# Key-value sums in four parts of 128 small matmuls, with MLP units between the parts, in a fused linear-attention and SwiGLU kernel

## The chip, the cores and the metric

The kernel runs on one core of a Trainium2 chip. The metric is device time in microseconds (us) of one execution; lower is better. Five engines work side by side, each through its own list of instructions in order: TensorE (PE in the profile; its weight loads are PEld), VectorE (DVE), ScalarE (ACT), GpSimd (POOL) and SyncE (SP), which here issues all DMA transfers.

## The reference

For one sequence of S = 2048 tokens with D = 640 features, two branches are added to the input. Both start from the same layer-normed input.

```python
xn = _layernorm(x)                     # x: (1, 2048, 640)
# branch A: linear attention, H = 32 heads of Dh = 20
q, k, v = split(xn @ wqkv)
pq = einsum("bhsd,hdf->bhsf", q, w_phi);  pk = einsum("bhsd,hdf->bhsf", k, w_phi)
phi_q = concat([softmax(pq), softmax(-pq)]);  phi_k = concat([softmax(pk), softmax(-pk)])
kv  = einsum("bhsf,bhsd->bhfd", phi_k, v);    z = einsum("bhsf->bhf", phi_k)
o   = einsum("bhqf,bhfd->bhqd", phi_q, kv) / (einsum("bhqf,bhf->bhq", phi_q, z) + 1e-6)
A   = o @ wo
# branch B: SwiGLU, F = 1536
B   = (silu(xn @ w1) * (xn @ w3)) @ w2
out = x + A + B
```

The key-value sums `kv` and `z` run over all tokens. Per head they are a matrix of 40 by 20 and a vector of 40.

## The kernel before

**Tiles.** Tokens lie in T = 16 tiles of 128 and in NB = 4 blocks of 512; D is cut into DC = 5 chunks of 128, F into FC = 12. Matrices are bf16, sums in PSUM are f32. PSUM has eight banks; every unit of work asks for one or two of them (`banks(n)`), those that become free first.

**Stages.** Layer norm and transposition of x; then, tile by tile, keys (with w_phi folded into the weights, `Wkp`) and values; the exponentials of the keys land in `ekt`, are summed on VectorE and scaled on GpSimd (`k_norm`); v is kept in `v2`, with a column of ones behind each head, so that z comes out of the same sums as kv. Then the key-value sums (`kv_sum`), their store into a block layout (`kv_store`, into `KVc`), and for every token tile `q_tok`: 40 small groups of matmuls against `KVc`, the division on VectorE, and a transposed DMA into `oT`. The query projections (`q_proj`) run a block ahead. The MLP is cut into 48 units (`mlp`, one block of tokens by one chunk of F): five matmuls for the gate and five for the up projection, each 128x512, in two banks; a tanh on ScalarE; two steps on VectorE, which leave the result in `hT` and free the banks. `out_tile` adds both branches in PSUM, 34 matmuls of 320 columns per token tile, and SP writes the tile out.

**The key-value sums.** Lines 554 to 565. Eight heads' columns n, 16 token tiles t and four row groups r give 8 x 16 x 4 = 512 matmuls in one unit. Each loads its own weights, 128 x 21 (a head of v and the column of ones), and streams 40 columns (both halves of `ekt` of this head). They go into 320 columns of one bank, and one ScalarE instruction (`kv_copy`) brings these to `stg`. In the profile the matmuls read `PS<-ekt,v`, that copy `stg<-PS,eps`, the MLP's matmuls `PS<-xnT,w_s` (w1 and w3; w2 has the name `w_s`, too), those of `q_proj` `PS<-xnT,Wqp`, those of `q_tok` `PS<-KVc,EqT`.

**What sets the order.** The program is planned before it is built. Each stream of work (norms, transposes, attention, MLP, outputs and so on, line 820) is a generator that yields units, or nothing while it has to wait. The planner (lines 823 to 858) keeps a modelled time for each engine, takes the unit that can start first by its model (`P.ready` for units with TensorE work), and appends its instructions to the engines' lists; a unit is never cut. The costs in the code (as 0.0055 per small matmul at line 563) serve this model alone. On the chip each engine goes through its list in order, and semaphores carry the dependences that `find_deps` found. The stream `attention` yields all projections, then `kv_masks`, `kv_sum` (line 781), `kv_store`, and the load of w2, which goes where `ekt` lay; MLP units of the last block wait for this (line 807).

Of the kernel before, what the change touches and what calls it, by code (L numbers as in the profile page):

```python
# [11 lines left out]
DH = 20  # L12
F = 1536
T = S // 128
# [232 lines left out]
def bass_parallel_sum__linear_kernel_hedgehog__glu_gated_swiglu__prompt_kernel(  # L247
# [10 lines left out]
):  # L258
    bf = DT.bfloat16
    LAG = 4.0  # L260
    f32 = DT.float32
    P = _Program(nc)

# [11 lines left out]
    def new(name, shape, dtype, offset=None):  # L275
        size = mybir.dt.size(dtype)
        for n in shape[1:]:
            size *= n
        return P.sbuf(name, shape, dtype, region(size) if offset is None else offset)
# [10 lines left out]
    eps = new("eps", [128, 8], f32)  # L290
# [43 lines left out]
    stg = new("stg", [128, 2, 160], bf, RW + 1344)  # L334
# [10 lines left out]
    def bank(k, cols=512, off=0, rows=128):  # L345
        return PS[0:rows, k * 512 + off:k * 512 + off + cols]
# [5 lines left out]
    def mm(o, l, r, start, stop, shared=False, cost=None):  # L352
        n = free(r)
        P.op("PE", "matmul", [o], [l, r], (o, l, r),
             dict(start=start, stop=stop, skip_group_check=shared),
             cost=max(n / 2400 + 0.003, 0.055) if cost is None else cost)
# [5 lines left out]
    def free(ap):  # L362
        n = 1
        for s in ap.shape[1:]:
            n *= s
        return n
# [132 lines left out]
    def fold_mm(which, dc, k):  # L499
        first = [True, True]  # L500
        for e in range(DC):
            h0, h1 = heads_of_chunk(e)
            lo, hi = DH * h0, DH * (h1 + 1)
            for q in range(2):
                a, b = max(lo, 320 * q), min(hi, 320 * q + 320)
                if a < b:
                    mm(bank(k + q, b - a, a - 320 * q), wqkT[:, which * DC + e, 128 * dc:128 * dc + 128],
                       BDc[:, e, a - lo:b - lo], first[q], e == DC - 1 or (q == 0 and e == 2), True)
                    first[q] = False
        if which:  # L510
            evac(Wkp[:, dc, :].rearrange("p (b c) -> p b c", c=320), bank2(k, 320))
        else:
            evac(Wqp[:, dc, :].rearrange("p (i b r j) -> p b r i j", b=2, r=2, j=32),
                 bank2(k, 320).rearrange("p b (r i j) -> p b r i j", r=2, j=32))
# [8 lines left out]
    def v_half(t, q, k):  # L523
        for i in range(DC):
            mm(bank(k, 320), xnT[:, i, t * 128:(t + 1) * 128], wv[:, i, 320 * q:320 * q + 320],
               i == 0, i == DC - 1)
        act(v2[:, t, 336 * q:336 * q + 336].rearrange("p (h c) -> p h c", c=21)[:, :, 0:DH],
            bank(k, 320).rearrange("p (h c) -> p h c", c=DH), ACT.Copy)

    def v_tile(t, k):  # L530
        proj(t, wv, k)
        pv = bank2(k, 320).rearrange("p b (h c) -> p b h c", c=DH)
        act(v2[:, t, :].rearrange("p (b h c) -> p b h c", b=2, c=21)[:, :, :, 0:DH], pv, ACT.Copy)

    def k_tile(t, k):
        proj(t, Wkp, k)
        pk = bank2(k, 320)
        for sg in range(2):
            act(ekt[:, t, sg, :].rearrange("p (b c) -> p b c", c=320), pk, ACT.Exp,
                1.0 if sg == 0 else -1.0)  # L540
# [10 lines left out]

    def kv_sum(k):
        for n in range(8):
            for t in range(T):
                for r in range(4):
                    h = 8 * r + n
                    o = PS[32 * r:32 * r + DH + 1, k * 512 + 40 * n:k * 512 + 40 * n + 40]
                    edge = r == 0 and (n == 0 and t == 0 or n == 7 and t == T - 1)  # L560
                    mm(o.rearrange("p (s f) -> p s f", s=2), v2[:, t, 21 * h:21 * h + DH + 1],
                       ekt[:, t, :, DH * h:DH * h + DH], t == 0, t == T - 1, True,
                       (0.1 if edge else 0.0) + 0.0055)
        kv_copy(stg[:].rearrange("p s (n f) -> p n s f", f=DH),
                bank(k, 320).rearrange("p (n s f) -> p n s f", s=2, f=DH), eps[:, 0:1])

    def kv_copy(o, i, e):
        n = free(o)
        P.op("ACT", "activation", [o], [i, e], (o, i, ACT.Identity), dict(bias=e), cost=0.17 + n / 1200)
# [22 lines left out]
    def q_proj(b, fc, k):  # L592
        for i in range(DC):
            mm(bank(k), Wqp[:, i, fc * 128:(fc + 1) * 128], xnT[:, i, b * 512:(b + 1) * 512],
               i == 0, i == DC - 1)
        act(EqT[b % 2][:, 0, fc, :], bank(k), ACT.Exp)
        act(EqT[b % 2][:, 1, fc, :], bank(k), ACT.Exp, -1.0)
# [51 lines left out]
    def load_xres(t):  # L649
        P.dma("SP", xres[:, t % 4, :], x_t[:, t, :])  # L650
# [23 lines left out]
    def banks(n):  # L674

        def free_at(k):
            return max([o.end for i in range(k, k + n) for o in P.bank.get(("P", i), {}).values()],
                       default=0.0)
        return min(range(0, 8, n), key=free_at)

    done = dict.fromkeys(("w", "ln", "t", "f", "k", "n", "kv", "q", "o", "h"), 0)
# [70 lines left out]
    def attention():  # L752
        def v(t):
            return lambda: v_tile(t, banks(2))

        yield warm_up
        for t in range(4):
            while done["t"] <= t:
                yield None
            for q in range(2):  # L760
                yield lambda t=t, q=q: v_half(t, q, banks(1))
        while done["f"] < 1:
            yield None
        for t in range(T):
            while done["t"] <= t:
                yield None
            yield lambda t=t: k_tile(t, banks(2))
            done["k"] = t + 1
            if t >= 4:
                yield v(t)  # L770
            if 9 <= t < 14:
                while done["f"] < 2:
                    yield None
                yield lambda dc=t - 9: fold_mm(0, dc, banks(2))
        yield lambda: P.dma("SP", wo_s[:], A_wo.rearrange("(c p) d -> p c d", p=128))
        for fc in range(DC):
            yield lambda fc=fc: q_proj(0, fc, banks(1))
        while done["n"] < T:
            yield None
        yield kv_masks  # L780
        yield lambda: kv_sum(banks(1))
        yield kv_store
        done["kv"] = 1
        yield lambda: P.dma("SP", w2_s[:], B_w2.rearrange("(c p) d -> p c d", p=128))
        yield lambda: (load_xres(0), load_xres(1))
        for b in range(NB):
            for j in range(4):
                t = 4 * b + j
                while done["o"] < t - 2:
                    yield None  # L790
                yield lambda t=t: q_tok(t, 0)
                done["q"] = t + 1
                if b + 1 < NB:
                    for fc in range((5 * j + 3) // 4, (5 * j + 8) // 4):
                        yield lambda b=b, fc=fc: q_proj(b + 1, fc, banks(1))
# [22 lines left out]
    MLPS = 7  # L818
    URGENT = {0: 4.0, 4: 4.0, 6: 4.0}
    streams = [norms(), transposes(), fold_k(), attention(), k_norms(), loads(), o_transposes(), mlps(), outs()]  # L820
    n = len(streams)
    heads, alive = [None] * n, [True] * n
    while any(alive):
        best = None
        for i in range(n):
            if heads[i] is None and alive[i]:
                s = next(streams[i], StopIteration)
# [12 lines left out]
            if any(o.eng == "PE" for o in ops):  # L840
                at = max(P.ready(ops), P.free["PE"] + 0.15)
                if i == MLPS and P.free["DVE"] > P.free["PE"] + LAG:
                    rank = n
# [10 lines left out]
        i, ops, after = best[2:]  # L854
# [65 lines left out]
```

## Time and profile before

| | us |
|---|---|
| median of 3 runs | 281.02 |
| lowest and highest run | 280.66, 281.38 |
| the profiled execution | 280.1 |
| its span, first to last instruction | 278.4 |
| mean granted TensorE clock in it | 0.988 |

A run's time is the span and 1.7 us around it. The profile is of one execution. Its rows give the engine, the operation, the tiles (output<-inputs), the shape, a count, the busy time and the mean length of one, and then the idle time of the engine just before these instructions, with what ended most of it; "issue" there is a wait for nothing that the profile shows. All instructions come from the helper at line 105, so groups are told apart by their tiles, not their lines. Matmuls are pipelined: one lasts longer than the distance to the next, so starts are counted, not lengths. Some records of matmuls are missing from a trace. The granted clock is TensorE's, 1.00 being full speed.

### The profile page before, as it was taken

What the parts mean: (1) busy time and instruction counts of PE and PEld (TensorE: products, weight loads), DVE (VectorE), ACT (ScalarE), POOL (GpSimd) and SP (SyncE); (2) the same over time, 40 slices, a digit from 0 to 9 for tenths busy, and PEclk for the clock granted to TensorE, in tenths of its full rate; (3) what the DMA queues carried; (4) which work ended last, traced back from release to release, by engine and by line L of the source; (5) the groups of instructions that cost most, each with busy time, mean ns of one, the idle gap of its engine ahead of it and who ended that gap; (6) DMA issues with size and microseconds to landing.
All of it is one profiled execution on the core that took longest, in us unless ns stands there. A gap on an engine that the chain in (4) does not pass through costs nothing.

```text
span 278.4 us, 6314 instructions
## 1 busy us (share of the span) xinstructions
PE 263.4 (95%) x2711; PEld 155.8 (56%) x2735; DVE 179.4 (64%) x306; ACT 104.7 (38%) x196; POOL 60.9 (22%) x99
## 2 busy tenths in 40 slices
PE   6999999999994599999999999999999999999996
PEld 2656666676444344444444444446666666777774
DVE  5469879999561066656666799994665555786212
ACT  2567988887720122232222355451223222100000
POOL 4405496999982000000000100000000000000000
PEclk9999999999999599999999999999999999999999
DMA  6972799630000270000000011120633432253311
GB/s 193 305 214 47 167 318 228 122 117 0 0 0 5 58 279 0 0 2 0 1 0 2 0 26 24 27 47 26 90 80 82 64 93 73 73 116 99 99 46 47
DMA packets 40332, 22.06 MB, mean 79 GB/s; under 512 B 26736, under 2 KB 40304, under 8 KB 40304
## 3 DMA queue, kind: packets, MB, share of 16 engines
q1 hardware_dynamic: 40304, 21.66, 31.8%
q8 instruction: 21, 0.34, 0.5%
q14 instruction: 7, 0.06, 0.1%
HBM read 12.81 MB, written 2.62 MB: 55 GB/s over the span
## 4 chain that ended last, share of the span: by engine, by line
PE 88%; issue 4%; DMA 4%; SPq 2%; DVE 1%; ACT 1%
PE PS L105 88%; DMA wqkT<-in_A_wqkv_dram 4%; SPq L117 2%; DVE S L105 1%; ACT Wkp L105 0%; ACT ekt L105 0%; DVE t L105 0%; DVE rS L105 0%; DVE xres L105 0%; DVE hT L105 0%
## 5 line engine op out<-in xcount | busy, mean ns | idle before, releaser
L105 PE MATMUL PS<-xnT,w_s 128*128 128x512 bf16 x469 | 105.1, 381 | 1.0 <-issue 0.3
L105 PEld LDWEIGHTS PS<-xnT,w_s 128*128 128x128 bf16 x480 | 47.1, 98 | 56.7 <-issue 1.4
L105 DVE SCALAR_TENSOR_TENSOR t<-th,PS 128x512 bf16<-128x512 f32 x48 | 32.8, 683 | 42.7 <-ACT th L105 42.4
L105 PE MATMUL PS<-w_s,hT 128*128 128x320 bf16 (+2 forms) x384 | 54.9, 299 | 0.0
L105 ACT ACTIVATE th<-PS 128x512 f32<-128x512 f32 x48 | 28.7, 599 | 58.7 <-PE PS L105 58.7
L105 PEld LDWEIGHTS PS<-w_s,hT 128*128 128x128 bf16 x384 | 37.6, 98 | 14.6
L105 POOL TENSOR_TENSOR ekt<-ekt,rS 128x640 bf16<-128x640 bf16 x32 | 39.4, 1272 | 4.1 <-DVE rS L105 4.1
L105 DVE TENSOR_TENSOR xres<-PS,xres 128x640 bf16<-128x640 f32 (+2 forms) x17 | 13.4, 786 | 38.9 <-PE PS L105 38.9
L105 DVE SCALAR_TENSOR_TENSOR hT<-t,PS 128x512 bf16<-128x512 bf16 x48 | 33.0, 687 | 1.7
L105 ACT ACTIVATE e_s<-PS 128x64 f32<-128x64 f32 x32 | 6.4, 283 | 52.2 <-PE PS L105 52.2
L105 PE MATMUL PS<-wv,xnT 128*128 128x320 bf16 x160 | 24.7, 299 | 1.0 <-ACT xnT L105 1.0
L105 ACT ACTIVATE EqT<-PS 128x512 bf16<-128x512 f32 x40 | 21.7, 594 | 9.2 <-PE PS L105 9.2
L105 PE MATMUL PS<-wo_s,oT 128*128 128x320 bf16 (+2 forms) x160 | 24.5, 299 | 0.0
L105 DVE TENSOR_TENSOR prod<-PS,g_s 128x1280 bf16<-128x1280 f32 x16 | 23.9, 1491 | 0.6
L105 PE MATMUL PS<-Wkp,xnT 128*128 128x320 bf16 x160 | 23.9, 299 | 0.1
L105 ACT ACTIVATE ekt<-PS 128x640 bf16<-128x640 f32 x32 | 20.9, 720 | 6.3 <-PE PS L105 6.3
L105 DVE TENSOR_REDUCE S<-ekt 128x64 f32<-128x1280 bf16 x16 | 23.1, 1441 | 0.0
L105 PE MATMUL PS<-xnT,Wqp 128*128 128x512 bf16 x87 | 20.9, 379 | 2.0 <-issue 1.9
L105 PEld LDWEIGHTS PS<-wv,xnT 128*128 128x128 bf16 x160 | 15.2, 98 | 7.5 <-ACT xnT L105 1.5
L105 PEld LDWEIGHTS PS<-wo_s,oT 128*128 128x128 bf16 x160 | 15.3, 98 | 7.2
L105 PEld LDWEIGHTS PS<-Wkp,xnT 128*128 128x128 bf16 x160 | 15.4, 98 | 6.5 <-issue 0.3
L105 DVE BATCH_NORM_STATS2 bst<-x_tok 128x6 f32<-128x320 bf16 x32 | 15.3, 478 | 4.9 <-DMA x_tok<-in_A_x_dram 4.3
(52 smaller groups left out, 142.9 us busy)
## 6 DMA issues: line engine op xcount, KB each, us to landing
w_s<-in_B_w_dram SPq DMA_DIRECT2D x6, 640.0 KB, 6.1
xres<-in_A_x_dram SPq DMA_DIRECT2D x16, 160.0 KB, 2.5
out_dram<-xres SPq DMA_DIRECT2D x15, 160.0 KB, 1.8
x_tok<-in_A_x_dram SPq DMA_DIRECT2D x3, 640.0 KB, 6.3
w_s<-in_B_w_dram SPq DMA_DIRECT2D x1, 1920.0 KB, 9.4
wv<-in_A_wqkv_dram SPq DMA_DIRECT2D x2, 400.0 KB, 4.8
wo_s<-in_A_wo_dram SPq DMA_DIRECT2D x1, 800.0 KB, 4.8
x_tok<-in_A_x_dram SPq DMA_DIRECT2D x4, 160.0 KB, 2.9
```

Source lines behind the costliest of these rows:

```text
L105: o = _Op(eng, lambda: m(*args, **kw), r, w, cost)
L117: o = _Op(eng, lambda: m(out, in_), self.regions(in_), self.regions(out), nbytes, True)
```

## The change

`kv_sum` is called four times, with m = 0 to 3, for the columns n = 2m and 2m + 1: 128 matmuls each, over all 16 token tiles and four row groups. Each part goes to 80 columns of whichever bank is free first, and has a copy of its own into its 40 columns of `stg`. Between two parts the attention stream yields nothing until the modelled TensorE time has gone on by 4.2 us (`KV_GAP`), as long as there are MLP units of the first three blocks. The modelled cost of one small matmul goes from 0.0055 to 0.008.

```diff
+    KV_GAP = 4.2
...
-    def kv_sum(k):
-        for n in range(8):
+    def kv_sum(m, k):
+        for n in (2 * m, 2 * m + 1):
             for t in range(T):
                 for r in range(4):
                     h = 8 * r + n
                     o = PS[32 * r:32 * r + DH + 1, k * 512 + 40 * n:k * 512 + 40 * n + 40]
-                    edge = r == 0 and (n == 0 and t == 0 or n == 7 and t == T - 1)
+                    edge = r == 0 and (n % 2 == 0 and t == 0 or n % 2 and t == T - 1)
                     mm(o.rearrange("p (s f) -> p s f", s=2), v2[:, t, 21 * h:21 * h + DH + 1],
                        ekt[:, t, :, DH * h:DH * h + DH], t == 0, t == T - 1, True,
-                       (0.1 if edge else 0.0) + 0.0055)
-        kv_copy(stg[:].rearrange("p s (n f) -> p n s f", f=DH),
-                bank(k, 320).rearrange("p (n s f) -> p n s f", s=2, f=DH), eps[:, 0:1])
+                       (0.1 if edge else 0.0) + 0.008)
+        i, o = bank(k, 80, 80 * m), stg[:, :, 40 * m:40 * m + 40]
+        kv_copy(o.rearrange("p s (n f) -> p n s f", f=DH),
+                i.rearrange("p (n s f) -> p n s f", s=2, f=DH), eps[:, 0:1])
...
         yield kv_masks
-        yield lambda: kv_sum(banks(1))
+        for m in range(4):
+            until = P.free["PE"] + KV_GAP
+            while m and P.free["PE"] < until and done["h"] < 3:
+                yield None
+            yield lambda m=m: kv_sum(m, banks(1))
         yield kv_store
```

On TensorE, from the end of the query projections of the first block to the first `q_tok`, the list is this (rows with - are those of before, rows with + of the changed kernel; ten `PS<-xnT,w_s` are one MLP unit):

```order
 L105 MATMUL PS<-xnT,Wqp 128x512 x25
 L105 MATMUL PS<-xnT,w_s 128x512 x50
-L105 MATMUL PS<-ekt,v_83 21x40 x512
-L105 MATMUL PS<-xnT,w_s 128x512 x300
+L105 MATMUL PS<-ekt,v_83 21x40 x128
+L105 MATMUL PS<-xnT,w_s 128x512 x20
+L105 MATMUL PS<-ekt,v_83 21x40 x128
+L105 MATMUL PS<-xnT,w_s 128x512 x20
+L105 MATMUL PS<-ekt,v_83 21x40 x128
+L105 MATMUL PS<-xnT,w_s 128x512 x20
+L105 MATMUL PS<-ekt,v_83 21x40 x128
+L105 MATMUL PS<-xnT,w_s 128x512 x230
```

Six of the thirty MLP units that followed the sums now stand between the parts, two in each place, and 23 come behind the last part: one unit fewer than before stands ahead of the first `q_tok`.

On ScalarE, at the same place, the copies of the sums stand between the tanh steps of the MLP units (in brackets the engines whose semaphores an instruction waits for):

```order
-L105 ACTIVATE stg<-PS,eps 128x8x2x20 [waits s_PE]
+L105 ACTIVATE stg<-PS,eps 128x2x2x20 [waits s_PE]
+L105 ACTIVATE th<-PS 128x512 [waits s_PE] x2
+L105 ACTIVATE stg<-PS,eps 128x2x2x20 [waits s_ACT,s_PE]
+L105 ACTIVATE th<-PS 128x512 [waits s_PE] x2
+L105 ACTIVATE stg<-PS,eps 128x2x2x20 [waits s_PE]
+L105 ACTIVATE th<-PS 128x512 [waits s_PE] x2
+L105 ACTIVATE stg<-PS,eps 128x2x2x20 [waits s_ACT,s_PE]
 L105 ACTIVATE th<-PS 128x512 [waits s_PE] x3
```

Each copy waits for its own part of the sums, and two of them for an earlier copy on the same engine; the tanh of the unit behind it comes after it in the list.

The unit that was left over comes out on TensorE after the fifth `q_tok`, in front of the sixth:

```order
 L105 MATMUL PS<-xnT,Wqp 128x512 x10
-L105 MATMUL PS<-xnT,w_s 128x512 x10
-L105 MATMUL PS<-wo_s,oT 128x320 x10
-L105 MATMUL PS<-w_s,hT_77 128x320 x24
+L105 MATMUL PS<-xnT,w_s 128x512 x20
 L105 MATMUL PS<-KVc,EqT_82 128x44 x4
```

There two MLP units stand instead of one and an output tile; from here on every output tile comes one place later, so that six of them instead of five follow the last `q_tok`. The lists of VectorE and SP move with this: the transposed DMA of the sixth `o_tok` is issued ahead of the first output tile's residual load and store.

## The prediction

> **What bounds the kernel now.** I read the page's first part and its chain, then the groups of instructions with shapes kept apart, and then, for the place the change touches, the timeline of TensorE and the windows of one microsecond.
>
> ```profile
> span 278.4 us, 6314 instructions
> PE 263.4 (95%) x2711; PEld 155.8 (56%) x2735; DVE 179.4 (64%) x306; ACT 104.7 (38%) x196; POOL 60.9 (22%) x99
> ...
> PE 88%; issue 4%; DMA 4%; SPq 2%; DVE 1%; ACT 1%
> ```
>
> TensorE sets the end: it is busy for 95% of the span and 88% of the last chain runs through it. So an edit is worth the time for which TensorE stands still or runs slowly because of it. The 4% of "issue" is time in which it waited for nothing that the profile shows. Most of that lies in one group, the 512 key-value matmuls:
>
> ```profile
> L105 PE MATMUL PS<-ekt,v 128*21 128x40 bf16 x512 | 4.9, 192 | 6.2 <-issue 6.2
> ```
>
> The timeline of TensorE puts this idle time in order (start, length, count, idle before):
>
> ```profile
> 79.75 3.83 PE L105 MATMUL PS<-xnT,w_s 128*128 128x512 bf16 x17
> 83.51 1.30 PE L105 MATMUL PS<-ekt,v 128*21 128x40 bf16 x141
> 86.21 1.19 PE L105 MATMUL PS<-ekt,v 128*21 128x40 bf16 x128 [1.39 <-issue]
> 89.66 1.21 PE L105 MATMUL PS<-ekt,v 128*21 128x40 bf16 x128 [2.26 <-issue]
> 93.39 1.15 PE L105 MATMUL PS<-ekt,v 128*21 128x40 bf16 x115 [2.52 <-issue]
> 94.87 6.45 PE L105 MATMUL PS<-xnT,w_s 128*128 128x512 bf16 x25 [0.33 <-issue]
> ```
>
> The sums run in bursts of exactly 128 pairs (a weight load and a matmul, 256 instructions) with 1.39, 2.26 and 2.52 us of nothing between them: 6.17 us. What TensorE waits for is seen in the instruction queue and in the windows (busy time by engine, then granted clock, DMA share, GB/s):
>
> ```profile
> q8 instruction: 21, 0.34, 0.5%
> ```
>
> ```profile
> 83.00:84.00 1.00, 1.00 (x68) 0.58 (x66) 0.79 (x2) 0.14 (x1) 0.79 (x4) 1.00 0.07 16
> ...
> 87.00:88.00 1.00, 0.40 (x48) 0.30 (x37) 0.00 (x0) 0.00 (x0) 0.00 (x0) 1.00 0.07 16
> 88.00:89.00 1.00, 0.00 (x0) 0.00 (x0) 0.00 (x0) 0.00 (x0) 0.00 (x0) 1.00 0.00 0
> 89.00:90.00 1.00, 0.34 (x47) 0.34 (x47) 0.00 (x0) 0.00 (x0) 0.00 (x0) 0.92 0.00 0
> 90.00:91.00 1.00, 0.87 (x104) 0.76 (x92) 0.00 (x0) 0.00 (x0) 0.00 (x0) 0.50 0.07 16
> ...
> 94.00:95.00 1.00, 0.67 (x66) 0.67 (x53) 0.00 (x0) 0.01 (x1) 0.00 (x0) 0.50 0.05 16
> ...
> 96.00:97.00 1.00, 1.00 (x4) 0.40 (x3) 0.00 (x0) 0.18 (x1) 0.00 (x0) 0.66 0.80 215
> ```
>
> 21 packets carry 0.34 MB, 16 KB each, and TensorE's 2711 + 2735 records over 21 packets are 259 instructions a packet: a packet is a block of about 256 instructions of TensorE. One microsecond with 16 GB/s is such a packet, and there is one shortly after the start of each burst and none between. So I read it thus: when TensorE's queue enters a block, the next one is fetched, and it can be used 3.45 us (86.21 to 89.66) to 3.73 us (89.66 to 93.39) after that. A block of large matmuls lasts far longer; a block of 128 small pairs is used up in 1.2 us, and TensorE waits out the rest.
>
> The Trainium skill says otherwise: "Runtime: NRT & Kernel Launch", section "Instruction fetch mechanics", has the same blocks of 256 instructions but calls the cost of crossing one mostly hidden. By that rule the three gaps would have another cause and would stay, which is the second rival below; the trace, with 2.26 and 2.52 us at distances of 128 pairs, does not agree.
>
> There is a second loss. The granted clock is 0.92 in the window 89 to 90, 0.50 until 96 and 0.66 in 96 to 97: half speed from 89.84 to 96.68. The small pairs hardly feel it (1.21 us against 1.19 for 128), the large matmuls behind them do.
>
> **The change, part by part.** First, the price of one large matmul and of the switch between kinds:
>
> ```profile
> 171.12 0.47 PE L105 MATMUL PS<-KVc,EqT 32*128 32x44 bf16 x40
> 171.74 1.03 PE L105 MATMUL PS<-xnT,Wqp 128*128 128x512 bf16 x4 [0.16 <-issue]
> 172.60 4.48 PE L105 MATMUL PS<-xnT,w_s 128*128 128x512 bf16 x20
> ```
>
> ```profile
> L105 PE MATMUL PS<-xnT,w_s 128*128 128x512 bf16 x469 | 105.1, 381 | 1.0 <-issue 0.3
> ...
> L105 PEld LDWEIGHTS PS<-xnT,w_s 128*128 128x128 bf16 x480 | 47.1, 98 | 56.7 <-issue 1.4 <-ACT Wkp L105 0.3
> ```
>
> One large matmul lasts 0.381, so 20 in 4.48 start every (4.48 - 0.38) / 19 = 0.2158 us. There are 480 weight loads but 469 matmul records: a record is missing here and there, and the "0.16" after the 40 small ones is such a place (4 of 5 recorded), so the first large one really began at 171.74 - 0.216 = 171.52. The 0.33 before 94.87 is the same: at half speed the one before it began at 94.87 - 0.43 = 94.44.
>
> What the sums cost now: 17 matmuls from 79.75 leave the next start at 79.75 + 17 x 0.2158 = 83.42. The next large matmul begins at 94.44: 11.02 us. Then 26 of them (25 recorded) end at 94.87 + 6.45 = 101.32; at full speed from 94.44 they would end at 94.44 + 25 x 0.2158 + 0.38 = 100.22: 1.10 us more. **Together 12.12 us** of TensorE.
>
> What they cost in four parts without waits: a burst of 128 lasts 1.19, and its last matmul about 0.19 (192 ns in the group), so its 127 steps take 1.00 (7.9 ns each; 141 in 1.30 give the same). Switching in takes 83.51 - 83.42 = 0.09. Switching out takes, after the 40 small ones that end at 171.12 + 0.47 = 171.59 and so begin the last at 171.40, 0.12. One part is 1.21 us, **four are 4.85**. The three extra switches, 3 x 0.21, are in this. Bounds for a part: 1.09 if switching out is free, 1.31 if it takes a large matmul's whole step of 0.216; four are 4.4 to 5.2.
>
> Whether the blocks now come in time: the first stall comes after pair 141 and the next 128 pairs later, so a block ends 13 pairs into the sums, and the next holds the other 115 pairs and 26 instructions of MLP, 13 matmuls. It was there at 86.21 and will be, since nothing ahead of it changes; TensorE needs it only when 13 of the 20 matmuls are done that begin at 83.42 + 1.21 = 84.63, at 87.43. The block after that is then asked for at 86.21 and is there 3.45 to 3.73 later, at 89.66 to 89.94. It is needed after the other 7 matmuls and 121 pairs: 84.63 + 20 x 0.2158 = 88.95, + 0.09 + 121 x 0.0079 = 89.99. So 0.05 to 0.33 us to spare, the tightest place. The two after that have a whole part and 20 matmuls, 5.5 us, for the same 3.7. I take no stall; the bound is the first rival.
>
> Whether the clock stays: with no idle time TensorE works on large matmuls for 20 x 0.216 = 4.3 us between two parts of 1.2. I take 1.00 throughout; that the 1.10 goes rests on it, and the third rival is the other case.
>
> What moves at no cost: the evacuation of the sums on ScalarE becomes four.
>
> ```profile
> 94.99 0.53 ACT L105 ACTIVATE stg<-PS,eps 128x320 bf16<-128x320 f32 x1 [11.85 <-PE PS L105]
> 96.82 0.60 ACT L105 ACTIVATE th<-PS 128x512 f32<-128x512 f32 x1 [1.30 <-PE PS L105]
> 98.99 0.60 ACT L105 ACTIVATE th<-PS 128x512 f32<-128x512 f32 x1 [1.57 <-PE PS L105]
> ```
>
> Each is at most the 0.53 of the large one. Behind it in ScalarE's queue stands the tanh of the next MLP unit, whose gate matmuls take 5 x 0.216 = 1.08 us from the same moment, so it hides; uncovered it would delay that tanh by at most 0.53, and ScalarE idles 1.57 per unit. The bank that a part holds is free 4.3 us before the next part. The store of the sums, the load of w2 (one issue of 1920 KB on SP, the residual loads queued behind it) and all that follows come some 7 us later than now, at about 101 us; the first reader of the sums starts at 160, that of w2 at 189. In the attention stretch one MLP unit comes later and one output tile moves behind the last q_tok. The same matmuls, so TensorE's sum is the same; the question is VectorE.
>
> ```profile
> 170.00:180.00 10.00, 9.68 (x121) 4.62 (x122) 9.39 (x18) 4.97 (x12) 0.00 (x0) 1.00 0.18 35
> ```
>
> Here VectorE is busy 9.39 of 10 and TensorE does not wait for it (its 0.32 of gaps are the two missing records). The piece that gains an MLP unit has the vector work of these pieces and five Wqp matmuls more on TensorE, so it is less tight.
>
> **The sum:** 12.12 - 4.85 = 7.27, say 7.3 us. The profiled execution took 280.1 (span 278.4): 272.8. The median of the three runs, 281.02, is 0.9 above it; against it the change gives 273.7, and that is my number.
>
> **The rivals.** (1) The block comes late once. If the queue runs no further ahead than TensorE itself, the tight block is asked for not at 86.21 but at 87.43, is there at 90.88 to 91.16, and TensorE stands 0.9 to 1.2 us before the end of the second part: 274.6 to 274.9. For it: 0.05 us of margin is little. Against it: the later packets show 0.6 to 1.8 us after their bursts' starts (87 to 88 after 86.21, 94 to 95 after 93.39), so that of 83 to 84 was asked for before 83.4, when TensorE had not begun the sums, 13 pairs ahead of the block's edge: the queue runs ahead.
>
> (2) The gaps belong to the small matmuls, not to the fetch (also the case in which the change doesn't do what it says). Then each part ends in or begins with its gap and only the clock is won: 1.10 - 0.63 = 0.5 us, 280.5. Against it: the packet at each burst.
>
> (3) Slower: the clock. If the clock is set by stretches of 3.42 us, half of the 6.84 at half speed, the one that ended at 89.84 held 0.97 + 0.18 = 1.15 us of small matmuls and the clock fell; the one before it held 2.0 us, of which 0.5 were large ones, and it stayed. If small matmuls count for so little that each part's stretch falls below the bound, all 60 matmuls between the parts run at half speed: 60 x 0.211 = 12.7 us lost, 286.4, slower from 35 such matmuls on (7.3 / 0.211). Against it: any 3.42 us now hold at least 3.42 - 1.21 = 2.2 us of large matmuls, four times the 0.5 that sufficed. The Trainium skill, "TensorE: Matmul & The Clock Gate", Part 1, says that the clock falls after a window of 3.4 us that is idle. By that rule a part could never trigger it; the trace agrees in the length (6.84 is two windows) but not in the "idle", as a third of that window was busy.
>
> **How the numbers follow.** Forecast, no stall to 0.3 of one: 0.78, with 272.8 to 274.4 by the own sum and the bounds of the switch. Rival 1: 0.11. Rival 2: 0.05. Rival 3: 0.02. Something that costs one to three microseconds elsewhere, in the attention stretch: 0.04. The range goes from 272.4, the profiled execution's 280.1 less the largest gain 12.12 - 4.4 = 7.7, to 275.5, the highest run 281.38 less 12.12 - 5.0, a part's upper bound all but reached, plus the 1.2 of rival 1. About 0.3%, 0.84 us, is what a measurement of this kernel can tell from no change. Faster: 0.93; within: 0.04 (rival 2 partly); slower: 0.03.
>
> **What would show it.** In the changed timeline four bursts of 128, each about 1.2 us, with 20 large matmuls of 4.48 between and no "issue" gap over 0.3 us; the granted clock 1.00 from 80 to 110; the packets of 16 GB/s spread over the MLP stretches, each before it is needed; the attention stretch as full as before. A gap in the second part alone is rival 1, gaps at every part rival 2, a clock of 0.50 with matmuls 0.43 apart rival 3. The prediction is wrong if the time is above 275.5.

## The result, and the profile after

The changed kernel takes 273.43 us (median of 4 runs, 273.33 to 274.11) against 281.11 (280.66 to 281.38) before: a ratio of 0.9734, 95% interval 0.9714 to 0.9754. That is 7.7 us less; 7.3 and 273.7 us had been forecast. A run more than 1.5% above the fastest of its kernel is taken for one in a slower state and left out of the ratios; among the runs below this holds for the 278.03 us of experiment 5 alone.

The page of the changed kernel, its first part, chain and the group of the sums:

```profile
span 272.4 us, 6311 instructions
PE 264.0 (97%) x2709; PEld 156.9 (58%) x2735; DVE 179.3 (66%) x306; ACT 105.6 (39%) x199; POOL 60.9 (22%) x99
...
PE 95%; issue 1%; DVE 1%; DMA 1%; ACT 0%
```

```profile
L105 PE MATMUL PS<-ekt,v 128*21 128x40 bf16 x512 | 4.9, 185 | 0.6 <-issue 0.6
```

The same 512 matmuls, busy for the same 4.9 us, now have 0.6 us of idle time before them instead of 6.2, and "issue" has left the chain but for 1%. The mean clock is 1.000 instead of 0.988. TensorE's timeline (start, length, count, idle before) shows where the 0.6 lies:

```profile
79.27 4.70 PE L105 MATMUL PS<-xnT,w_s 128*128 128x512 bf16 x21
83.90 1.20 PE L105 MATMUL PS<-ekt,v 128*21 128x40 bf16 x128
85.25 4.26 PE L105 MATMUL PS<-xnT,w_s 128*128 128x512 bf16 x19 [0.16 <-issue]
89.44 1.14 PE L105 MATMUL PS<-ekt,v 128*21 128x40 bf16 x121
91.22 0.22 PE L105 MATMUL PS<-ekt,v 128*21 128x40 bf16 x7 [0.64 <-issue]
91.60 4.26 PE L105 MATMUL PS<-xnT,w_s 128*128 128x512 bf16 x19 [0.16 <-issue]
95.79 1.19 PE L105 MATMUL PS<-ekt,v 128*21 128x40 bf16 x128
97.15 4.26 PE L105 MATMUL PS<-xnT,w_s 128*128 128x512 bf16 x19 [0.16 <-issue]
101.34 1.20 PE L105 MATMUL PS<-ekt,v 128*21 128x40 bf16 x128
102.69 7.50 PE L105 MATMUL PS<-xnT,w_s 128*128 128x512 bf16 x34 [0.16 <-issue]
```

Three parts run through in 1.2 us. The second stands still for 0.64 us after pair 121, the place that the prediction had called the tightest. The four gaps of 0.16 are missing records (19 of 20 in the first three). By starts, the stretch from 83.81 (the last large matmul before the sums begins at 79.27 + 4.70 - 0.38 = 83.59, and a step is 0.22) to 102.69 - 0.216 = 102.47 holds 60 large matmuls, 12.95 us; the rest, 5.71 us, is the price of the sums. 12.12 had been counted for before: 6.4 less. The profiled executions are 6.0 apart (280.1 and 274.11), since this one came 0.39 us later to the sums (83.90 against 83.51): in it, the first five matmuls of the values, `PS<-wv,xnT`, took 1.52 us instead of 0.85.

### The profile page after: what moved, and what is told of

Read it like the earlier page. It is cut to its first block, busy times and chain, and to the rows that moved or that the text cites. A ratio compares the mean times of both kernels' runs of the same rounds, so it can differ in the third digit from the quotient of the medians.

```text
span 272.4 us, 6311 instructions
## 1 busy us (share of the span) xinstructions
PE 264.0 (97%) x2709; PEld 156.9 (58%) x2735; DVE 179.3 (66%) x306; ACT 105.6 (39%) x199; POOL 60.9 (22%) x99
## 4 chain that ended last, share of the span: by engine, by line
PE 95%; issue 1%; DVE 1%; DMA 1%; ACT 0%
PE PS L105 95%; DMA x_tok<-in_A_x_dram 1%; DVE bst L105 1%; ACT xnT L105 0%; DVE xres L105 0%; DVE mv L105 0%; DVE x_tok L105 0%
## 5 line engine op out<-in xcount | busy, mean ns | idle before, releaser
L105 PEld LDWEIGHTS PS<-xnT,w_s 128*128 128x128 bf16 x480 | 46.5, 98 | 55.2 <-ACT Wkp L105 0.2
L105 PE MATMUL PS<-wv,xnT 128*128 128x320 bf16 x160 | 25.7, 309 | 0.8 <-ACT xnT L105 0.8
L105 PEld LDWEIGHTS PS<-wv,xnT 128*128 128x128 bf16 x160 | 15.8, 101 | 7.7 <-ACT xnT L105 1.1
```

Source lines behind the costliest of these rows:

```text
L105: o = _Op(eng, lambda: m(*args, **kw), r, w, cost)
```

## The experiments

Theory A is the prediction's: instructions of TensorE come in blocks of 256, and the next one can be used 3.45 to 3.73 us after its predecessor was entered. Theory B is the prediction's second rival in a definite form: small matmuls stop by themselves after a number of their kind.

**1. Four parts without MLP units between them.**

```diff
             until = P.free["PE"] + KV_GAP
-            while m and P.free["PE"] < until and done["h"] < 3:
-                yield None
```

> The changed kernel without the pause between the parts: four parts of 128, four banks' pieces and four copies, back to back, all MLP units behind them. Theory A: the parts are worth nothing by themselves, bursts of 141, 128, 128, 115 and gaps of about 1.4, 2.3, 2.5 us with half the clock after them as before: 280.6 to 281.6 us. If the cut into parts (banks, copies, one unit less at a time) is what counts, under 277 us.

280.99 us (10 runs), ratio 0.9982 (0.9958 to 1.0006). TensorE's timeline of this kernel:

```profile
83.92 1.30 PE L105 MATMUL PS<-ekt,v 128*21 128x40 bf16 x141
87.20 1.19 PE L105 MATMUL PS<-ekt,v 128*21 128x40 bf16 x128 [1.98 <-issue]
90.93 1.25 PE L105 MATMUL PS<-ekt,v 128*21 128x40 bf16 x128 [2.54 <-issue]
94.38 1.15 PE L105 MATMUL PS<-ekt,v 128*21 128x40 bf16 x115 [2.20 <-issue]
```

The same bursts of 141, 128, 128 and 115 as before, though a part ends after each 128: the gaps don't follow the parts, and the cut, the banks and the copies are worth nothing by themselves. All of the gain is in what stands between the parts.

**2. Two parts of 256.**

```diff
     def kv_sum(m, k):
-        for n in (2 * m, 2 * m + 1):
+        for n in range(4 * m, 4 * m + 4):
...
-        for m in range(4):
+        for m in range(2):
             until = P.free["PE"] + KV_GAP
```

(The lines left out make the columns of the bank and of the staging tile twice as many, and move the marks of a part's first and last matmul.)

> Two parts of 256 pairs with two MLP units between. Theory A: a gap of about 1.4 us after pair 141 of the first part, none at its end, then gaps in the second part after pairs 121 (0.6 to 1.2 us) and 249 (2.2 to 2.6 us): 276 to 279 us, between the two kernels. Theory B: each part has its one gap at the same pair, 141 or 128, 275 to 277 us.

278.86 us (277.38 to 281.0, 4 runs), ratio 0.9894 (0.9849 to 0.9939). TensorE's timeline:

```profile
83.41 1.30 PE L105 MATMUL PS<-ekt,v 128*21 128x40 bf16 x141
86.99 1.08 PE L105 MATMUL PS<-ekt,v 128*21 128x40 bf16 x115 [2.28 <-issue]
88.00 4.49 PE L105 MATMUL PS<-xnT,w_s 128*128 128x512 bf16 x20
92.42 1.14 PE L105 MATMUL PS<-ekt,v 128*21 128x40 bf16 x121
94.17 1.19 PE L105 MATMUL PS<-ekt,v 128*21 128x40 bf16 x128 [0.61 <-issue]
97.90 0.25 PE L105 MATMUL PS<-ekt,v 128*21 128x40 bf16 x7 [2.54 <-issue]
```

The gaps stand after pairs 141, 121 and 249, as theory A had counted them from instruction numbers: 115 pairs and 13 large matmuls, then 7 and 121 pairs, fill a block of 256. A number of small matmuls (theory B) gives no such pattern. The first gap was 2.28 us instead of 1.4; experiment 4 comes back to it. The four runs lie far apart, and in the order of their mean clocks: 277.38 us at 1.000, 278.43 and 279.30 at 0.994, and 281.0, the profiled one, at 0.988.

**3. One MLP unit between the parts.**

```diff
-    KV_GAP = 4.2
+    KV_GAP = 2.1
```

> The changed kernel with one MLP unit between the parts. Theory A: 276 instructions (128 pairs and 10 large matmuls with their loads) now take 3.4 us of TensorE, less than the 3.45 to 3.73 us that a block takes to come, and the edges fall at pair 3 of the second part, behind the third or fourth large matmul after it, at pair 121 of the third part and pair 111 of the fourth. So gaps return, one of them of 0.5 to 2.2 us amid the LARGE matmuls, together 1.7 to 4.2 us: 274.7 to 277 us. Theory B (small matmuls stop by themselves): never a gap amid large ones, and none in parts of 128: 273.0 to 273.5 us.

275.74 us (4 runs), ratio 0.9811 (0.9781 to 0.984). TensorE's timeline, from the end of the first unit on:

```profile
86.67 1.20 PE L105 MATMUL PS<-ekt,v 128*21 128x40 bf16 x128
88.02 0.59 PE L105 MATMUL PS<-xnT,w_s 128*128 128x512 bf16 x2 [0.16 <-issue]
90.20 1.67 PE L105 MATMUL PS<-xnT,w_s 128*128 128x512 bf16 x7 [1.58 <-issue]
91.80 1.14 PE L105 MATMUL PS<-ekt,v 128*21 128x40 bf16 x121
93.65 0.22 PE L105 MATMUL PS<-ekt,v 128*21 128x40 bf16 x7 [0.72 <-issue]
```

This speaks against theory B: TensorE stops for 1.58 us behind the third large matmul (two recorded and one missing), in the middle of a unit, where the profile shows nothing that it waits for. By the count of instructions the edge of a block lies there. The blocks come 3.45 us apart (90.20 to 93.65). The gaps, 1.58 and 0.72, and the time lie in the ranges of theory A.

**4. Where the edges lie.** First, the kernel before with 20 more small matmuls in the warm-up, which moves all edges 20 pairs forward:

```diff
+        for _ in range(5):
+            for i in range(4):
+                mm(bank(i, 66), z[32 * i:32 * i + 32, 0:128], z[32 * i:32 * i + 32, 0:66], True, True, cost=0.0)
```

> The kernel before, with 20 more small matmuls (40 instructions with their weight loads) in the warm-up at the very start, where TensorE waits for x. The sums themselves are untouched. Theory A: every edge of a block moves 20 pairs forward in the sums, so the bursts are 121, 128, 128, 128 and a rest of 7 pairs: four gaps instead of three, the first of 0.9 to 1.4 us, the others 2.2 to 2.6, together 7.5 to 8.9 instead of 6.17; with the longer half speed 282.3 to 284 us. Theory B: bursts of 141, 128, 128, 115 as before, 281.1 us.

281.83 us (10 runs), ratio 1.0015 (0.9989 to 1.0041). TensorE's timeline, and below it the windows (columns as before) with the packets of the blocks:

```profile
82.90 2.20 PE L105 MATMUL PS<-ekt,v 128*21 128x40 bf16 x249
87.18 1.21 PE L105 MATMUL PS<-ekt,v 128*21 128x40 bf16 x128 [2.08 <-issue]
90.64 1.25 PE L105 MATMUL PS<-ekt,v 128*21 128x40 bf16 x128 [2.24 <-issue]
94.64 0.25 PE L105 MATMUL PS<-ekt,v 128*21 128x40 bf16 x7 [2.75 <-issue]
```

```profile
77.00:78.00 1.00, 1.00 (x6) 0.47 (x5) 0.49 (x1) 0.39 (x1) 1.00 (x2) 1.00 0.09 16
84.00:85.00 1.00, 1.00 (x132) 1.00 (x121) 0.00 (x0) 0.00 (x0) 0.23 (x1) 1.00 0.06 16
```

The edges moved to 249, 377 and 505, but that at 121 cost nothing: the expectation missed there, and the time stayed the same. The packet for the block behind it came in 77 to 78, five us before the sums. The edge at which this packet is asked for now lies 13 instructions ahead of the first sums; in the kernel before it lay 27 behind their start, and the packet came in 83 to 84. So TensorE's queue runs far ahead, but here it did not get past the first sums early. What may hold it there is a wait: the last thing that these need is the memset of v's columns of ones on GpSimd (start, length; first the kernel before, then the changed one in its first profile, then in a second one):

```profile
80.43 2.37 POOL L105 MEMSET v<- 128x512 bf16 x1
```

```profile
81.42 2.37 POOL L105 MEMSET v<- 128x512 bf16 x1
```

```profile
80.57 2.37 POOL L105 MEMSET v<- 128x512 bf16 x1
```

It ends at 82.80, 83.79 and 82.94 (start and length added), and the packet comes in 83 to 84, 85 to 86 and 84 to 85. The second profile of the changed kernel is that of this run:

> The changed kernel once more. Theory A (TensorE's instructions come in blocks of 256, and the next block can be used 3.45 to 3.73 us after its predecessor was entered): the gap in the second part stands after pair 121, where a block ends, or is absent; where it is absent the span is 0.7 to 0.9 us shorter than the 272.4 us of the first profile, and a span near 271.6 shows no gap. Theory B (small matmuls stop by themselves after a number of their kind): the gap is there in every execution, at the same pair, and the 0.8 us between executions come from elsewhere. Both: 273.4 us, 0.972 to 0.975 of the kernel before.

273.12 us (272.76 to 274.08, 6 runs), ratio 0.9713 (0.9684 to 0.9742). Its timeline at the second part has no gap, in a span of 271.3:

```profile
89.24 1.20 PE L105 MATMUL PS<-ekt,v 128*21 128x40 bf16 x128
90.37 4.49 PE L105 MATMUL PS<-xnT,w_s 128*128 128x512 bf16 x20
```

The windows of the first profile, 84 to 93 us, show the late chain there: the packet in 85 to 86, the next in 88 to 89, the gap, and the one after it:

```profile
85.00:86.00 1.00, 0.84 (x16) 0.51 (x6) 0.00 (x0) 0.33 (x1) 0.79 (x4) 1.00 0.06 16
...
88.00:89.00 1.00, 1.00 (x7) 0.47 (x5) 0.35 (x1) 0.53 (x1) 0.00 (x0) 1.00 0.06 16
...
90.00:91.00 1.00, 0.58 (x70) 0.49 (x59) 0.51 (x1) 0.00 (x0) 0.00 (x0) 1.00 0.00 0
...
92.00:93.00 1.00, 1.00 (x6) 0.49 (x5) 0.00 (x0) 0.34 (x1) 0.00 (x0) 1.00 0.06 16
```

The same times for the kernel before, experiments 1 and 2 and three profiles of the changed kernel, the third from experiment 6 (packets to 0.1 us):

| | memset ends | sums begin | packet | gap |
|---|---|---|---|---|
| before | 82.80 | 83.51 | 83.8 | 1.39, after pair 141 |
| experiment 1 | 83.67 | 83.92 | 84.8 | 1.98, after pair 141 |
| experiment 2 | 82.88 | 83.41 | 84.6 | 2.28, after pair 141 |
| changed, first | 83.79 | 83.90 | 85.4 | 0.64, in part 2 |
| changed, second | 82.94 | 83.69 | 84.0 | none |
| changed, third | 83.21 | 83.29 | 84.4 | 0.20, in part 2 |

In the first three rows the block is used about 2.4 us after the start of its packet (86.21, 87.20 and 86.99). Two things move the packet. One is when GpSimd is done, against TensorE: the second part of the changed kernel has its gap where the sums begin 0.11 or 0.08 us after the memset's end, and none where they begin 0.75 after it. The other is the time from the memset's end to the packet, 1.0 to 1.7 us, and no run shows what sets it: in experiment 2, whose memset ends 0.08 us later than before, it makes 0.7 of the 0.9 us by which the first gap is longer.

**5. The memset taken out of the way.**

```diff
+    def ones():
         memset("POOL", v2[:].rearrange("p t (h c) -> p t h c", c=21)[:, :, :, DH], 1.0)
...
         yield block_diag
+        yield ones
```

(The line of the memset now belongs to `ones`, a unit near the start, and no more to `consts_late`, the last unit of this stream.)

> The changed kernel, with the memset of v's columns of ones moved on GpSimd from behind the last key tiles to the start, behind the masks of the folded weights. Theory A2 (the block that the second part needs is asked for late because the first sums wait for this memset, and TensorE's queue can't pass an instruction that waits): the packet that came 1.1 us after the memset's end now comes 1.5 to 4 us before the sums begin, no gap in any part, and no execution with the extra 0.8 us: spans 270.8 to 271.6, 272.6 to 273.3 us. Rival (the gap depends on how long a single fetch takes by chance): the packet comes where it did, and one execution in three or four still has a span above 272. A third case: GpSimd's 2.4 us at the start delay the layer norm, 274 us or more.

274.54 us (273.47 to 278.03, 6 runs), ratio 0.975 (0.9725 to 0.9775): the third case. No part has a gap of its own, and the packet comes at 83.6 for sums that begin at 85.14, 1.5 us ahead, as expected. What the sums wait for last on GpSimd is now the last scaling of `ekt`:

```profile
69.87 12.33 POOL L105 TENSOR_TENSOR ekt<-ekt,rS 128x640 bf16<-128x640 bf16 x10
```

It ends at 82.20, and the packet comes 1.4 us after it, as it came 1.0 to 1.7 after the memset: the packet went with the end of the wait and not with the start of the sums. That is the best evidence here that the queue doesn't pass a waiting instruction. The time does not show it: the sums begin 1.2 to 1.5 us later than in the first two profiles of the changed kernel. A part of this isn't the edit's, since in this execution, too, the first five matmuls of the values took 1.51 us instead of 0.85, before the memset began at 14.60. The rest is not settled, nor why the median is 1 us above the changed kernel's.

**6. A longer pause, and the edges moved in the changed kernel.**

```diff
-    KV_GAP = 4.2
+    KV_GAP = 6.3
```

> The changed kernel with three MLP units between the parts instead of two. Theory A: each block has 2.2 us more to come, no gap in any part, 272.6 to 273.3 us, the executions with an extra 0.8 us gone. If longer pauses cost something (the banks, VectorE in the attention stretch), 274 us or more.

272.98 us (272.65 to 273.83, 6 runs), ratio 0.9705 (0.9682 to 0.9728), no gap in any part. Then the diff of experiment 4 with 12 in the place of 5, that is 48 more small matmuls, on the changed kernel:

> The changed kernel with 48 more small matmuls in the warm-up at the start, which move every edge of a block 48 pairs forward: to pairs 93, 73, 53 and 33 of the four parts, each with the same 2.9 to 5.5 us or more since the block before was entered, and the first of these blocks asked for ahead of the first sums' wait. Theory A: no gap in any part, 272.6 to 273.5 us. Theory B: as the changed kernel.

272.34 us (271.96 to 272.72, 4 runs), ratio 0.9684 (0.9657 to 0.971), no gap in any part, and faster than expected. Either the moved edges or the longer warm-up could do it, so a longer warm-up alone, the 48 once more, and the 48 with three units between the parts ran beside the changed kernel on one chip. The version with nine large matmuls instead of seven lengthens the warm-up, in its profile until 6.37 us (5.35 in the changed kernel's, 6.10 with the 48), and moves the edges by two pairs only (two more large matmuls behind the seven, at no modelled cost).

> The changed kernel, as the base for the three beside it: 272.8 to 273.6 us by either theory.

> The changed kernel with nine large warm-up matmuls at the start instead of seven; the edges of the blocks move by 2 pairs only. Theory W (the gain of the version with 48 more small warm-up matmuls, 272.34 against some 273.1, comes from the start: a longer warm-up brings the full clock before the first tiles in more executions): 272.3 to 272.7 us, while the gap in the second part may stay in some executions. Theory E (it comes from the moved edges alone): 272.9 to 273.6 us, as the changed kernel, or more for the time of the two matmuls.

> The changed kernel with 48 more small warm-up matmuls once more, beside the changed kernel: 272.0 to 272.7 us, no gap in any part. Should it not be faster than the changed kernel beside it, the earlier 272.34 was chance.

> Both at once: 48 more small warm-up matmuls and three MLP units between the parts. Theory A: there is no gap left for the longer pause to remove, so as the version with two units, 272.0 to 272.7 us.

| on one chip | median us (range) | ratio to before | sums begin at | gap in part 2 |
|---|---|---|---|---|
| changed kernel | 273.60 (273.04 to 274.53) | 0.9723 (0.9696 to 0.9749) | 83.29 | 0.20 |
| nine large warm-up matmuls | 273.28 (273.17 to 273.67) | 0.9714 (0.9687 to 0.9741) | 83.70 | none (the part takes 1.28 instead of 1.20) |
| 48 more small ones | 272.66 (272.02 to 272.75) | 0.9684 (0.9657 to 0.9711) | 82.66 | none |
| 48 more, three units | 272.46 (272.07 to 272.76) | 0.9679 (0.9652 to 0.9706) | 83.24 | none |

The version with 48 more beats both kernels: six runs of it and of the changed kernel, and its slowest lies under the other's fastest, though the intervals of the two ratios to before overlap a little. The pause adds nothing to it that these runs can tell. The longer warm-up alone does not give it, so theory W falls. TensorE's timeline of that version, the second part:

```profile
88.20 1.20 PE L105 MATMUL PS<-ekt,v 128*21 128x40 bf16 x128
89.33 4.49 PE L105 MATMUL PS<-xnT,w_s 128*128 128x512 bf16 x20
```

Between these two profiles, 1.0 us apart in span (271.3 and 270.3), the stretch from the sums' start to the first large matmul behind them is 0.38 us shorter (17.76 against 18.14), and the sums begin 0.63 us earlier. The first is the gap. The second is there long before the sums, where the keys' folded weights are made (first the changed kernel, then the version with 48 more, then that with 48 more and three units):

```profile
16.87 1.76 PE L105 MATMUL PS<-BDc,wqkT 128*128 128x140 bf16 x30 [0.36 <-DMA wqkT<-in_A_wqkv_dram]
```

```profile
16.23 1.86 PE L105 MATMUL PS<-BDc,wqkT 128*128 128x140 bf16 x30
```

```profile
16.82 1.76 PE L105 MATMUL PS<-BDc,wqkT 128*128 128x140 bf16 x30 [0.31 <-DMA wqkT<-in_A_wqkv_dram]
```

One execution waited for a load there and the other did not. The third has the same list on TensorE up to the sums as the second; it waited, and its sums begin at 83.24. So in these profiles most of the 0.63 us come from a load's arrival and not from edges. Why none of the 15 runs with the 48 lies above any of the 16 of the changed kernel (they meet at 272.76) stays open: the medians are 0.9 us apart, and the gap is 0.38 of it in this pair of profiles.

## Why the prediction was right

- **The gaps are blocks of instructions that come late**: right. Their places follow instruction numbers through five different orders (141, 121 and 249, the third large matmul of a unit), and a pause of large matmuls removes them. The rule of the Trainium skill that crossing a block is mostly hidden ("Runtime: NRT & Kernel Launch", "Instruction fetch mechanics") holds here for large matmuls, whose 45.3 us from 94.87 on in the kernel before show no gap after the first, and not for these: 128 small pairs last 1.2 us, a block 3.45 to 3.73.
- **12.12 us for the sums before**: right for the profiled execution, low for the mean. Of the 45 runs of the kernel before beside the experiments, 20 have a mean clock of 0.987 or 0.988 and a median of 280.68 us, 20 have 0.981 or 0.982 and 281.95, five have 0.976 and 282.13. The list of cores of the profiled execution before, and of experiment 1:

```profile
core 0: 278.4 us, clock 0.988
```

```profile
core 0: 280.1 us, clock 0.982
```

(1 - 0.988) x 278.4 / 0.5 is 6.7 us at half speed, (1 - 0.982) x 280.1 / 0.5 is 10.1: two stretches of 3.4 us, or three. The prediction took the 0.9 us between the profiled execution and the median for something that the change leaves, but a third stretch, 3.4 x 0.5 = 1.7 us in about half of the runs, goes with the rest. So the gain by the medians (7.7 to 8.4) is above 7.3. That by the two profiles, 6.0, is below it, for the gap in part 2 and the later start.
- **4.85 us for four parts**: right where no gap is. In the second profile the stretch goes from 83.60 (the large matmuls before the sums, from 77.77 on, last 5.99; less the last one's 0.38, and a step of 0.22) to 101.46: 17.86 less 12.95 are 4.91.
- **No stall**: the step that failed in part. The prediction gave the second part 0.05 to 0.33 us to spare, and assumed that the block before it would come at the same moment as before, "since nothing ahead of it changes". By experiments 4 and 5 the block is asked for when the wait of the first sums ends, and this moved by 0.99 us between the profiled executions (82.80, 83.79); the packet came 1.6 us later. So rival 1 came true nearly in size (0.64 idle; 0.82 from the last start, 90.40, to the next, where it had 0.9 to 1.2) in one execution, and not in another. Its reason, a queue that runs no further ahead than TensorE, was wrong: the queue ran ahead by some 5 us (experiment 4), but in no profile past this wait.
- **That the number is so near is in part luck**: the gap, which the sum left out, made some executions longer by up to 0.8 us, and the third stretch at half speed, which it left out, too, made the gain larger. The one hides the other in the 0.3 us between 273.7 and 273.43.
- **The clock stays at 1.00**: right in 15 of 16 runs of the changed kernel, with 1.000; one shows 0.994 and is the slowest, 274.53, and no profile shows where. Rival 3, with 12.7 us, is out for this spacing.
- **The copies on ScalarE, the later store, the moved MLP unit cost nothing**: right. The group of the copies on the page, with the shapes apart:

```profile
L105 ACT ACTIVATE stg<-PS,eps 128x80 bf16<-128x80 f32 x4 | 1.3, 328 | 7.8 <-PE PS L105 7.8
```

Four of 0.33 us each, under the 1.08 us of the gate matmuls. In the attention stretch VectorE is busier than before (27.62 of these 30 us against 26.10) and TensorE still doesn't wait (window of the changed kernel, 150 to 180):

```profile
150.00:180.00 30.00, 29.21 (x324) 13.92 (x328) 27.62 (x51) 14.94 (x33) 0.00 (x0) 1.00 0.12 23
```

The 0.79 us missing there are five gaps of 0.16, one behind each q_tok, where a record is lost.

## What to carry to other kernels

Idle time of TensorE that is put down to "issue" and recurs every 128 pairs of weight load and matmul was late instructions here. Where you see it, spread the small matmuls among large ones, so that 256 instructions last at least the 3.7 us that a block took to come; two units of ten 128x512 per 128 pairs did it but for one edge in some executions, one unit did not. The edges of the blocks can be counted from the bursts and placed: with an edge 13 instructions ahead of a waiting one the block was there in time, with the edge 27 behind the packet came only 1.0 to 1.7 us after the wait's end. And look at the clock behind such pauses: three of 1.4 to 2.5 us between bursts of 1.2 also cost it, for 6.8 or 10.2 us, while the single 1.58 us of experiment 3 did not.

## What was not expected of the hardware

- TensorE's queue had a block fetched five us ahead of its use (77 to 78 for sums from 82.90) and then ran 249 small pairs without a gap, but where the edge lay behind the first sums, the packet came only after the end of their wait in all profiles.
- The clock fell after stretches that were not idle. In experiment 2 this is seen in the window 96 to 97 (0.85, so half speed began at 96.70):

```profile
96.00:97.00 1.00, 0.00 (x0) 0.00 (x0) 0.00 (x0) 0.00 (x0) 0.00 (x0) 0.85 0.52 61
```

If the clock goes by stretches of 3.42 us, as the prediction worked out from the 6.84 us at half speed, then in the one before, 93.28 to 96.70, TensorE was busy with small pairs for 0.28 + 1.19 = 1.47 us. In the kernel before the clock stayed with 2.0 of 3.42, of which 0.5 were large. What it counts, and where the bound lies between the two, no run shows.
